# Steps, order and places of the weight conversions in a kernel of sliding-window attention and two MLPs

## The chip, the cores and the metric

The kernel runs on one core of a Trainium2 chip. Its engines work side by side, each through its own list of instructions in order: TensorE (PE) multiplies matrices, VectorE (DVE) and ScalarE (ACT) do elementwise work, SyncE (SP) issues the transfers (DMA). An instruction starts when the one before it on its engine has started its way through and the semaphores that it waits for are set. The metric is the time of one execution in device microseconds (us).

## The reference

```python
def _attn_ref(q, k, v):                     # 4 batches, 8 heads, 576 positions, 64 a head
    scores = scale * np.matmul(q, k.transpose(0, 1, 3, 2))
    mask_plain = (rel >= 0) & (rel < 32)                              # heads 0 to 3
    mask_dil = (rel >= 0) & (rel < 128) & (rel % 4 == 0)              # heads 4 to 7
    ...
    attn = np.exp(scores - max); attn = attn / (sum + 1e-09)
    return np.matmul(attn, v)

def _moe_ref(x, w_in, w_out, s, b):         # 2304 tokens, 512 -> 2048 -> 512
    r = np.maximum(x @ w_in, 0.0)
    return (s * (r * r) + b) @ w_out

def _moe2_ref(x, w_in, w_out):
    h = x @ w_in
    return (h * np.cos(h)) @ w_out
```

The attention's output, as rows of 512 numbers for each of the 2304 tokens, goes through the first MLP (`_moe_ref`) and its result through the second (`_moe2_ref`). The weights are float64 as drawn.

## The kernel before

**Tiles and steps.** The tokens lie in five tiles of 384, 384, 512, 512 and 512. The hidden 2048 numbers are 16 chunks of 128; each chunk has an in-half (128x512 of the first matrix: half 2f) and an out-half (half 2f + 1). One step p takes one chunk of one tile: p = 0 to 79 the first MLP, tile by tile, p = 80 to 159 the second. In a step TensorE makes h of the chunk (`mm_in`), then y of the chunk of two steps ago (`mm_out`); between them lie relu2 (ScalarE twice, then VectorE twice, for an exact split of its result into a high and a low part) or the cosine of the second MLP. Every product of the later tiles is three matmuls (high with high, high with low, low with high); the first tile of the first MLP is done with plain float32 matmuls on the converted weights.

**Attention.** There are 48 units (192 tokens by a pair of heads). The first eight are done in a prelude; the rest in pairs, woven into the steps of the first MLP. A pair begun at step p has its scores at the start of p, its softmax behind y at p (VectorE L238, L247, then ScalarE's exponentials L250), its normalisation at p + 1 (VectorE L261 to L263), its transposes on TensorE at the end of p + 1 (L271), and its product with v (L283) at the end of p + 2. Pairs are begun at 3, 6, 9, 12; 16, 18, 21, 23, 26, 28; 32, 34, 37, 39, 42, 44; 49, 52, 56, 59 (`DUO`).

**Weights.** A half arrives as float64 words (512 KB) in a raw place. `w_float` makes float32 of it with two ScalarE passes (L117, L118), `w_join` with four operations of VectorE (L124, L127, L130, L133). I call the two together a conversion. For the first MLP, `w_whole` does conversions in the order 0, 1, 2, ... of the halves, two a step, in the first tile (`w_point`: up to 2p + 4 at the first point of step p, behind `mm_in`, and 2p + 5 at the second, behind `mm_out`); five raw places (`stage`) are loaded three ahead. `w_split` then makes the high and the low part, a half at a time (ScalarE L139, VectorE L140), in-halves from step 13 on, out-halves from step 16 on. For the second MLP a half is loaded, converted one step later and cut into its high and low part one step after that (`w_cut`: ScalarE L147, VectorE L148, two transfers to HBM, L149 and L150), at steps spread evenly over the tiles 1 to 4; `w_fetch` brings the parts back in the last tile, the in-half at step 64 + f and the out-half at 66 + f (L155, L156).

**What sets the order.** Nothing is scheduled by a planner: under `manual_schedule` each engine's list is the order in which the code emits. In a step that is `mm_in`, the events of phase 0 (scores, normalisations), y of a tile's last chunk, `w_point` (0), relu2 or cosine, `mm_out`, `w_point` (1), fetches, events of phase 1 (softmax), of phase 2 (transposes, products with v). The second MLP's loads, conversions and cuts are events of phase 1 or 2, whichever their evenly spread position falls in, and come behind a pair's in the same phase.

Of the kernel before, what the change touches and what calls it, by code (L numbers as in the profile page):

```python
# [54 lines left out]
def attention_then_two_mlps(ctx, tc, qk_p, qk_d, v_p, v_d, mask_p, mask_d, w1, w2, sv, bv, out):  # L55
# [41 lines left out]
    def w_load(m, k, stage):  # L100
        raw_w[m, k] = stage
        nc.sync.dma_start(stage[:, :DM], (w1, w2)[m][k])

    def w_float(m, k):
        words = raw_w[m, k][:, :DM].bitcast(U32).rearrange("p (n two) -> p n two", two=2)
        low, high = words[:, :, 0], words[:, :, 1]
        if m == 0 and k + 2 < 2 * NFC:
            a = wpool.tile([P, DM], I32, tag=f"wl{k + 2}", name=f"wa{m}_{k}")
        elif m == 0:
            if not last_two:  # L110
                last_two.append(wpool.tile([P, 2, DM], I32, tag="raw2", name="last_two"))
            a = last_two[0][:, k % 2, :]
        else:
            a = late[0].tile([P, DM], I32, tag=f"wa{k % 2}", name=f"wa{m}_{k}")
        w32[m, k] = a
# [4 lines left out]
    def w_join(m, k):  # L120
        words = raw_w[m, k][:, :DM].bitcast(U32).rearrange("p (n two) -> p n two", two=2)
        low, high = words[:, :, 0], words[:, :, 1]
        a = w32[m, k]
# [19 lines left out]
    def w_cut(k):  # L143
        a = w32.pop((1, k))
        hi = raw_w.pop((1, k)).bitcast(F32R)[:, :DM]
        cut[k] = scratch.tile([P, 2, DM], F32, tag=f"cut{k}", name=f"cut{k}")
# [2 lines left out]
        nc.sync.dma_start(cut[k][:, 0, :], hi.bitcast(F32))  # L149
        nc.sync.dma_start(cut[k][:, 1, :], a.bitcast(F32))  # L150

    def w_fetch(k):
        wh[1, k] = wpool.tile([P, DM], F32R, tag=f"wh{k}", name=f"wh1_{k}")
        wl[1, k] = wpool.tile([P, DM], F32R, tag=f"wl{k}", name=f"wl1_{k}")
        nc.sync.dma_start(wh[1, k].bitcast(F32), cut[k][:, 0, :])  # L155
        nc.sync.dma_start(wl[1, k].bitcast(F32), cut[k][:, 1, :])  # L156
# [20 lines left out]
    def a_load_first(i, what):  # L177
# [6 lines left out]
        place = lambda n, shape: wpool.tile(  # L184
            shape, F32, tag=("wh", "wl")[(5 * i + n) % 2] + str(2 * NFC - 1 - (5 * i + n) // 2), name=f"first{n}_{i}"
        )
        d["place"] = place
# [493 lines left out]
```

## Time and profile before

| what | before |
|---|---|
| median of 3 runs | 925.08 us (923.73 to 925.69) |
| the profiled execution | 924.52 us, its span 922.7 us |
| TensorE busy | 895.6 us, 97% of the span |
| VectorE busy | 590.2 us, 64% |
| ScalarE busy | 507.5 us, 55% |
| HBM read and written | 75.71 and 23.07 MB |

The times in the rows below are microseconds from the start of the span. The prelude ends near 30 us, the first tile near 123, the first MLP near 515. In the chain of work that ended last, 88% of the span is TensorE's and 7% VectorE's. A bracket at a row's end is the idle time of its engine just before it, with what ended it; a row without one followed straight on.

### The profile page before, as it was taken

The numbers are of one execution on the slowest core, as the hardware profiler recorded it, in microseconds if no ns is written. First come the engines' busy times: TensorE is split into PE (matmuls) and PEld (weight loads), VectorE is DVE, ScalarE is ACT, GpSimd is POOL, SyncE is SP. The second block draws the span as 40 slices with busy tenths as digits, with TensorE's granted clock in tenths as the row PEclk, the third lists the DMA queues.
The fourth block names the chain that finished last, engine by engine and source line by source line (L and its number), as shares of the span: only waits on it lengthen the run. The fifth ranks groups of instructions, "written<-read, shape, count | busy, mean of one in ns | idle before, by whom it ended". The sixth has DMA issues, their size and how long they took to land.

```text
span 922.7 us, 13285 instructions
## 1 busy us (share of the span) xinstructions
PE 895.6 (97%) x4888; PEld 755.4 (82%) x4888; DVE 590.2 (64%) x1160; ACT 507.5 (55%) x1162; POOL 0.7 (0%) x6
## 2 busy tenths in 40 slices
PE   6899999989999989999999999999999999999998
PEld 5566679889888877778888899999988888888886
DVE  6888868666565665557464766665755665566554
ACT  5767757666564654546353654645544554454443
POOL 0000000000000000000000000000000000000000
PEclk9799999999999999999999999999999999999999
DMA  9767424332534433436799700000000010001001
GB/s 261 245 224 241 138 72 156 105 119 88 173 129 138 143 122 125 156 101 215 251 319 309 256 16 1 20 16 1 20 15 1 1 45 1 1 1 47 0 1 46
DMA packets 45536, 99.64 MB, mean 108 GB/s; under 512 B 5440, under 2 KB 12064, under 8 KB 45472
## 3 DMA queue, kind: packets, MB, share of 16 engines
q1 hardware_dynamic: 45472, 98.80, 32.1%
q8 instruction: 39, 0.64, 0.3%
q14 instruction: 25, 0.20, 0.1%
HBM read 75.71 MB, written 23.07 MB: 107 GB/s over the span
## 4 chain that ended last, share of the span: by engine, by line
PE 88%; DVE 7%; ACT 3%; issue 1%; DMA 0%; SPq 0%; DVEq 0%
PE h L332 13%; PE h L333 13%; PE h L334 13%; PE y L349 12%; PE y L350 12%; PE y L351 12%; PE y L346 4%; PE h L326 4%; PE sc L220 2%; PE pv L283 2%; ACT sm L250 2%; PE tp L271 1%; DVE wa L133 1%; DVE wa L130 1%; DVE nmax L247 1%
## 5 line engine op out<-in xcount | busy, mean ns | idle before, releaser
L332 PE MATMUL h<-xs,wh 128*128 128x512 f32 (+1 forms) x576 | 218.6, 379 | 0.0
L349 PE MATMUL y<-g,wh 128*128 128x512 f32 (+1 forms) x576 | 214.9, 373 | 0.0
L333 PE MATMUL h<-xs,wh 128*128 128x512 f32 (+1 forms) x576 | 214.9, 373 | 0.0
L334 PE MATMUL h<-xs,wl 128*128 128x512 f32 (+1 forms) x576 | 214.8, 373 | 0.0
L351 PE MATMUL y<-g,wl 128*128 128x512 f32 (+1 forms) x576 | 213.7, 371 | 0.0
L350 PE MATMUL y<-g,wh 128*128 128x512 f32 (+1 forms) x576 | 213.6, 371 | 0.0
L332 PEld LDWEIGHTS h<-xs,wh 128*128 128x128 f32 x576 | 109.0, 189 | 15.7
L334 PEld LDWEIGHTS h<-xs,wl 128*128 128x128 f32 x576 | 108.8, 189 | 15.3
L333 PEld LDWEIGHTS h<-xs,wh 128*128 128x128 f32 x576 | 109.0, 189 | 14.8
L351 PEld LDWEIGHTS y<-g,wl 128*128 128x128 f32 x576 | 108.1, 188 | 15.1
L349 PEld LDWEIGHTS y<-g,wh 128*128 128x128 f32 x576 | 108.2, 188 | 14.8
L350 PEld LDWEIGHTS y<-g,wh 128*128 128x128 f32 x576 | 108.1, 188 | 14.7
L416 ACT ACTIVATE n<-n 128x512 f32<-128x512 f32 (+1 forms) x80 | 47.2, 590 | 102.5 <-DVE n L410 102.3
L406 ACT ACTIVATE n<-h,pmagic 128x512 f32<-128x512 f32 (+1 forms) x80 | 51.6, 646 | 87.0 <-PE h L334 86.9
L407 DVE TENSOR_SCALAR n<-n 128x512 f32<-128x512 f32 (+1 forms) x80 | 32.0, 400 | 86.6 <-ACT n L406 86.5
L422 DVE SCALAR_TENSOR_TENSOR n<-n,h 128x512 f32<-128x512 f32 (+1 forms) x80 | 50.7, 633 | 55.2 <-ACT n L417 55.2
L390 ACT ACTIVATE r<-h 128x512 f32<-128x512 f32 (+1 forms) x80 | 44.1, 551 | 67.3 <-PE h L334 58.8
L250 ACT ACTIVATE sm<-sm,nmax 96x80 f32<-96x80 f32 (+1 forms) x140 | 49.5, 355 | 46.1 <-DVE nmax L247 46.1
L400 DVE CAST g<-r 128x512 fp32r<-128x512 f32 (+1 forms) x64 | 26.1, 408 | 69.0 <-ACT r L398 59.5
L124 DVE TENSOR_SCALAR wa<-wa 128x512 f32<-128x512 f32 x62 | 26.2, 423 | 42.4 <-ACT wa L117 39.7
L410 DVE SCALAR_TENSOR_TENSOR n<-n,r 128x512 f32<-128x512 f32 (+1 forms) x80 | 51.1, 638 | 2.8
L409 DVE SCALAR_TENSOR_TENSOR r<-n,h 128x512 f32<-128x512 f32 (+1 forms) x80 | 50.7, 634 | 2.8
(81 smaller groups left out, 1060.6 us busy)
## 6 DMA issues: line engine op xcount, KB each, us to landing
stage<-w SPq DMA_DIRECT2D x32, 512.0 KB, 4.7
raw<-w SPq DMA_DIRECT2D x32, 512.0 KB, 4.6
cut<-raw SPq DMA_DIRECT2D x32, 256.0 KB, 2.1
cut<-wa SPq DMA_DIRECT2D x32, 256.0 KB, 2.5
wh<-cut SPq DMA_DIRECT2D x32, 256.0 KB, 3.9
wl<-cut SPq DMA_DIRECT2D x32, 256.0 KB, 4.4
qk<-qk_d SPq DMA_DIRECT2D x20, 352.0 KB, 3.4
qk<-qk_p SPq DMA_DIRECT2D x20, 304.0 KB, 2.9
```

Of the source, the lines that this page charges most:

```text
L250: nc.scalar.activation(out=sm[:, j, :], in_=sm[:, j, :], func=AF.Exp, bias=nmax[:, j : j + 1], scale=1.0, accum_out=ssum[:, j : j + 1],)
L332: nc.tensor.matmul(h[:, : SIZES[t]], hi, x[:, 0, :], start=cc == 0, stop=False)
L333: nc.tensor.matmul(h[:, : SIZES[t]], hi, x[:, 1, :], start=False, stop=False)
L334: nc.tensor.matmul(h[:, : SIZES[t]], lo, x[:, 0, :], start=False, stop=cc == NCC - 1)
L349: nc.tensor.matmul(y[:, : SIZES[t]], hi, g[:, 0, :], start=fc == 0, stop=False)
L350: nc.tensor.matmul(y[:, : SIZES[t]], hi, g[:, 1, :], start=False, stop=False)
L351: nc.tensor.matmul(y[:, : SIZES[t]], lo, g[:, 0, :], start=False, stop=fc == NFC - 1)
L406: nc.scalar.activation(out=n, in_=h[:, : SIZES[t]], func=AF.Identity, scale=1.0 / TWO_PI, bias=pmagic)
L409: nc.vector.scalar_tensor_tensor(out=r, in0=n, scalar=-C1, in1=h[:, : SIZES[t]], op0=ALU.mult, op1=ALU.add)
L410: nc.vector.scalar_tensor_tensor(out=n, in0=n, scalar=-C2, in1=r, op0=ALU.mult, op1=ALU.add)
L416: nc.scalar.activation(out=r, in_=r, func=AF.Sin, scale=0.5)
L422: nc.vector.scalar_tensor_tensor(out=r, in0=r, scalar=-1.0, in1=h[:, : SIZES[t]], op0=ALU.add, op1=ALU.mult)
```

## The change

1. Order of the first MLP's conversions: the in-halves of the first three chunks, then out-half f together with in-half f + 3 (`W_ORDER`), still two a step and to the same counts at each point. An in-half is so converted earlier in the list, an out-half later.
2. Nine raw places (five of `stage` and the four tiles that later hold a split x) instead of five, loaded five ahead.
3. Prelude: a unit's transposes and product with v come one iteration earlier, and the loop is one shorter; the first conversion stands behind the last transposes. The three memsets of g go to the kernel's start.
4. Weight tiles hold a whole chunk. `w1_split` splits it in one ScalarE and one VectorE operation of 128x1024, at step 14 + f, ahead of relu2; 16 such splits instead of 32 of half the width. The attention's first tiles lie in the high parts' tiles.
5. The second MLP's conversions are begun in written-out steps (`BG_STEPS`), none of which begins a pair: 19, 22, 25, 30; 33, 35, 36, 38, 40, 41, 45, 47; 48, 50, 51, 53, 54, 55, 57, 58, 61, 63; 64 to 70, 72, 73, 74. Before they were 19, 23, 26, 30; 33, 35, 37, 39, 41, 43, 45, 47; 48, 50, 52, 53, 55, 56, 58, 60, 61, 63; 64, 66, 68, 69, 71, 72, 74, 76, 77, 79, of which 23, 26, 37, 39, 52 and 56 begin a pair. The load is at phase 0 of the step before, the conversion at phase 1, the cut at phase 0 of the next step, ahead of relu2.
6. A chunk's fetch is two transfers of 512 KB at step 66 + f.

```diff
-W_FIRST, W_STEPS = (7, 8, 9, 10), {8: 1, 9: 2, 11: 3}
+W_FIRST, W_STEPS = (7, 8, 9, 10), {9: 1, 10: 3}
-AHEAD = 3
+AHEAD = 5
-IN_CUT = 13
+W_ORDER = [0, 2, 4] + [k for f in range(NFC) for k in (2 * f + 1, 2 * f + 6) if k < 2 * NFC]
+CUT = 14
...
+BG_STEPS = ((), (3, 6, 9, 14), (1, 3, 4, 6, 8, 9, 13, 15), (0, 2, 3, 5, 6, 7, 9, 10, 13, 15), (0, 1, 2, 3, 4, 5, 6, 8, 9, 10))
...
-    def w_split(k):
-        a = w32.pop((0, k)).bitcast(F32)
-        wh[0, k] = wpool.tile([P, DM], F32R, tag=f"wh{k}", name=f"wh0_{k}")
-        wl[0, k] = wpool.tile([P, DM], F32R, tag=f"wl{k}", name=f"wl0_{k}")
-        nc.scalar.copy(wh[0, k], a)
-        nc.vector.tensor_tensor(out=wl[0, k], in0=a, in1=wh[0, k].bitcast(F32), op=ALU.subtract)
+    def w1_load(n, k):
+        place, tag = (stage, f"s{n % 9}") if n % 9 < 5 else (xspool, f"xs{n % 9 - 5}")
+        raw_w[k] = place.tile([P, DM], I64, tag=tag, name=f"stage{k}")
+        nc.sync.dma_start(raw_w[k], w1[k])
...
+    def w1_split(fc):
+        a = flat(w32.pop(fc)).bitcast(F32)
+        wh[0, fc] = wpool.tile([P, 2, DM], F32R, tag=f"wh{fc}", name=f"wh0_{fc}")
+        wl[0, fc] = wpool.tile([P, 2, DM], F32R, tag=f"wl{fc}", name=f"wl0_{fc}")
+        nc.scalar.copy(flat(wh[0, fc]), a)
+        nc.vector.tensor_tensor(
+            out=flat(wl[0, fc]), in0=a, in1=flat(wh[0, fc]).bitcast(F32), op=ALU.subtract
+        )
...
+    def w2_fetch(fc):
+        for w, n, l in ((wh, 0, "wh"), (wl, 1, "wl")):
+            w[1, fc] = wpool.tile([P, 2, DM], F32R, tag=f"{l}{fc}", name=f"{l}1_{fc}")
+            nc.sync.dma_start(w[1, fc].bitcast(F32), cut[fc][:, n])
...
-        def w_whole(n):
+        def w_whole(n, more=1):
...
-            while q[2] < n:
-                while q[1] < min(q[2] + 2, 2 * NFC):
+            while q[2] < n or q[1] < min(n + more, 2 * NFC):
+                while q[1] < min(q[2] + 1 + more, n + more, 2 * NFC):
                     w_load_to(q[1] + 1)
-                    w_float(0, q[1])
+                    w1_float(W_ORDER[q[1]])
                     q[1] += 1
-                w_join(0, q[2])
-                q[2] += 1
+                if q[2] < n:
+                    w1_join(W_ORDER[q[2]])
+                    q[2] += 1
...
-        for k in range(n0 + 4):
+        for k in range(n0 + 3):
             if k < n0:
                 a_scores(k, ps_a)
                 a_softmax(k)
             if 0 <= k - 1 < n0:
                 a_norm(k - 1)
+            if 0 <= k - 2 < n0:
+                a_transpose(k - 2, ps_a)
             if 0 <= k - 3 < n0:
-                a_transpose(k - 3, ps_a)
-            if 0 <= k - 4 < n0:
-                a_pv(k - 4, ps_y, f"y{k % NCC}")
+                a_pv(k - 3, ps_y, f"y{k % NCC}")
...
-                w_whole(int(W_PACE * (p + half / 2)) + WPRE)
-            if half == 0 and 0 <= p - IN_CUT < NFC:
-                w_split(2 * (p - IN_CUT))
-            if half == 1 and 0 <= p - NFC < NFC:
-                w_split(2 * (p - NFC) + 1)
+                w_whole(2 * p + half + WPRE)
+            if half == 0 and 0 <= p - CUT < NFC:
+                w1_split(p - CUT)
...
-                at((p - 1, ph), load)
-                at((p, ph), lambda k=k: w_float(1, k))
-                at((p, ph), lambda k=k: w_join(1, k))
-                at((p + 1, ph), lambda k=k: w_cut(k))
+            at((p - 1, 0), lambda k=k: w2_load(k))
+            at((p, 1), lambda k=k: w2_float(k))
+            at((p, 1), lambda k=k: w2_join(k))
+            at((p + 1, 0), lambda k=k: w2_cut(k))
...
-            f = p - NFC * (NTILE - 1)
+            f = p - NFC * (NTILE - 1) - LAG[0]
             if 0 <= f < NFC:
-                w_fetch(2 * f)
-            if 0 <= f - LAG[0] < NFC:
-                w_fetch(2 * (f - LAG[0]) + 1)
+                w2_fetch(f)
```

VectorE at the end of the prelude, before: the last row of a unit's normalisation, copies of transposes (L273) and the first two conversions (L124 to L133, on the tiles wa_0 and wa_1).

```order
L263 TENSOR_TENSOR first_7_346<-first_7_346,rec_374 96x320
L273 COPY first_5_383<-tp_378 80x384
L124 TENSOR_SCALAR wa_0_395<-wa_0_395 128x512
L127 TENSOR_SCALAR wa_0_395<-wa_0_395 128x512
L130 SCALAR_TENSOR_TENSOR wa_0_395<-stage_154,wa_0_395 128x512
L133 ISA wa_0_395<-stage_154,wa_0_395 128x1024
L273 COPY first_6_412<-tp_407 80x384
L124 TENSOR_SCALAR wa_1_398<-wa_1_398 128x512
L127 TENSOR_SCALAR wa_1_398<-wa_1_398 128x512
L130 SCALAR_TENSOR_TENSOR wa_1_398<-stage_158,wa_1_398 128x512
L133 ISA wa_1_398<-stage_158,wa_1_398 128x1024
L273 COPY first_7_438<-tp_433 80x384
```

VectorE at the same place after: normalisation (L287), copies (L297), first conversion (L112 to L121, on wa_395, which is the in-half of chunk 0).

```order
L285 TENSOR_SCALAR ssum_350<-ssum_350 96x4
L286 RECIPROCAL rec_375<-ssum_350 96x4
L287 TENSOR_TENSOR first_qk_147<-first_qk_147,rec_375 96x320
L297 COPY first_v_158<-tp_379 80x384
L297 COPY first_v_162<-tp_402 80x384
L112 TENSOR_SCALAR wa_395<-wa_395 128x512
L115 TENSOR_SCALAR wa_395<-wa_395 128x512
L118 SCALAR_TENSOR_TENSOR wa_395<-stage_152,wa_395 128x512
L121 ISA wa_395<-stage_152,wa_395 128x1024
```

The copies for the last two units stood behind the first and the second conversion; now both stand ahead of the first.

VectorE in step 26, where a pair is begun, before: maxima of the softmax (L247), the conversion of a half of the second MLP, and the first unit's normalisation (L261 to L263), which belongs to step 27.

```order
L247 TENSOR_REDUCE nmax_1992<-sm_1990 96x4
L238 SCALAR_TENSOR_TENSOR sm_1999<-sc_1955,m_d 96x320
L247 TENSOR_REDUCE nmax_2001<-sm_1999 96x4
L124 TENSOR_SCALAR wa_2_2008<-wa_2_2008 128x512
L127 TENSOR_SCALAR wa_2_2008<-wa_2_2008 128x512
L130 SCALAR_TENSOR_TENSOR wa_2_2008<-raw_1935,wa_2_2008 128x512
L133 ISA wa_2_2008<-raw_1935,wa_2_2008 128x1024
L261 TENSOR_SCALAR ssum_1994<-ssum_1994 96x4
L262 RECIPROCAL rec_2028<-ssum_1994 96x4
L263 TENSOR_TENSOR sm_1990<-sm_1990,rec_2028 96x320
```

VectorE at the same pair after.

```order
L271 TENSOR_REDUCE nmax_1916<-sm_1914 96x4
L262 SCALAR_TENSOR_TENSOR sm_1923<-sc_1878,m_d 96x320
L271 TENSOR_REDUCE nmax_1925<-sm_1923 96x4
L285 TENSOR_SCALAR ssum_1918<-ssum_1918 96x4
L286 RECIPROCAL rec_1945<-ssum_1918 96x4
L287 TENSOR_TENSOR sm_1914<-sm_1914,rec_1945 96x320
```

The four operations between the second maximum and the normalisation are gone from this place; they are at step 25.

SyncE in the last tile of the first MLP, before, in some one and a half steps: cut (L149, L150), fetches by halves (L155, L156), load of a raw half (L102).

```order
L149 DMA cut_4652<-raw_4563 128x512
L150 DMA cut_4652<-wa_24_4604 128x512
L155 DMA wh_12_4695<-cut_3533 128x512
L156 DMA wl_12_4696<-cut_3533 128x512
L155 DMA wh_9_4699<-cut_3218 128x512
L156 DMA wl_9_4700<-cut_3218 128x512
L102 DMA raw_4703<-w 128x512
L149 DMA cut_4705<-raw_4611 128x512
L150 DMA cut_4705<-wa_25_4657 128x512
```

SyncE at a like place after: load (L156), fetches by chunks (L179), cuts (L173, L174).

```order
L179 DMA wh_1_4446<-cut_1887 128x1024
L179 DMA wl_1_4448<-cut_1887 128x1024
L173 DMA cut_4421<-raw_4373 128x512
L174 DMA cut_4421<-wa_25_4450 128x512
L156 DMA raw_4474<-w 128x512
L179 DMA wh_2_4494<-cut_2400 128x1024
L179 DMA wl_2_4496<-cut_2400 128x1024
L173 DMA cut_4518<-raw_4426 128x512
L174 DMA cut_4518<-wa_26_4498 128x512
L156 DMA raw_4523<-w 128x512
```

Four fetches of 256 KB a step became two of 512 KB, and in steps that follow each other there is a load and a cut in each.

## Rows read from the trace of the kernel before

**Rows 1.** The page: busy time of TensorE, share of the span.

```profile
PE 895.6 (97%) x4888; PEld 755.4 (82%) x4888; DVE 590.2 (64%) x1160; ACT 507.5 (55%) x1162; POOL 0.7 (0%) x6
```

**Rows 2.** Waits of TensorE, whole span: total us, times, longest us.

```profile
PE tp L271 <- DVE ssum L261: 8.2, 4, 2.8
...
PE tp L271 <- DVE sm L263: 2.0, 7, 0.4
```

**Rows 3.** TensorE's timeline, the four long waits: start, duration, instruction, idle before.

```profile
174.47 0.50 PE L271 MATMUL tp<-ident,sm 96*80 96x96 f32 x4 [1.77 <-DVE ssum L261]
...
193.81 0.50 PE L271 MATMUL tp<-ident,sm 96*80 96x96 f32 x4 [2.84 <-DVE ssum L261]
...
344.63 0.62 PE L271 MATMUL tp<-ident,sm 128*96 128x128 f32 x3 [2.35 <-DVE ssum L261]
...
392.97 0.50 PE L271 MATMUL tp<-ident,sm 96*80 96x96 f32 x4 [1.29 <-DVE ssum L261]
```

**Rows 4.** VectorE's timeline around the pair of step 26.

```profile
190.41 0.43 DVE L124 TENSOR_SCALAR wa<-wa 128x512 f32<-128x512 f32 x1 [2.58 <-ACT wa L117]
...
192.78 0.16 DVE L261 TENSOR_SCALAR ssum<-ssum 96x4 f32<-96x4 f32 x1
...
193.99 0.49 DVE L263 TENSOR_TENSOR sm<-sm,rec 96x320 f32<-96x320 f32 x1
```

**Rows 5.** ScalarE at step 26; VectorE and ScalarE at the cut in step 49.

```profile
189.74 0.65 ACT L117 ACTIVATE wa<-raw 128x512 f32<-128x512 f32 x1
...
343.01 0.69 DVE L148 TENSOR_TENSOR wa<-wa,raw 128x512 fp32r<-128x512 f32 x1 [1.98 <-ACT raw L147]
...
342.38 0.60 ACT L147 CAST raw<-wa 128x512 fp32r<-128x512 f32 x1
```

**Rows 6.** Windows: stretch, PE, PEld, DVE, ACT, POOL busy, clock, DMA share, GB/s.

```profile
190.00:195.00 5.00, 1.85 (x13) 1.38 (x12) 4.24 (x12) 3.33 (x7) 0.00 (x0) 0.97 0.00 0
195.00:200.00 5.00, 5.00 (x32) 4.99 (x30) 2.78 (x7) 2.62 (x6) 0.00 (x0) 0.69 0.28 105
...
345.00:350.00 5.00, 4.83 (x18) 3.81 (x17) 3.45 (x7) 1.21 (x3) 0.00 (x0) 0.67 0.07 24
```

**Rows 7.** VectorE's timeline, from the end of the prelude to the first pair.

```profile
22.92 0.55 DVE L273 COPY first<-tp 80x384 f32<-80x384 f32 x1
23.51 0.43 DVE L124 TENSOR_SCALAR wa<-wa 128x512 f32<-128x512 f32 x1
...
29.57 0.41 DVE L124 TENSOR_SCALAR wa<-wa 128x512 f32<-128x512 f32 x1
...
51.18 0.45 DVE L238 SCALAR_TENSOR_TENSOR sm<-sc,m_p 128x288 f32<-128x288 f32 x1
...
54.86 0.46 DVE L263 TENSOR_TENSOR sm<-sm,rec 128x288 f32<-128x288 f32 x1
```

**Rows 8.** TensorE's timeline, the first h and the first pair's transposes.

```profile
30.78 9.72 PE L326 MATMUL h<-xy,wa 128*128 128x384 f32 x24
...
54.60 0.49 PE L271 MATMUL tp<-ident,sm 128*96 128x128 f32 x3
55.46 0.51 PE L271 MATMUL tp<-ident,sm 128*96 128x128 f32 x3 [0.37 <-DVE sm L263]
```

**Rows 9.** The last tile: a window, and ScalarE's timeline (a load's wait, relu2 of two steps).

```profile
500.00:510.00 10.00, 10.00 (x46) 8.28 (x45) 5.72 (x11) 5.20 (x9) 0.00 (x0) 1.00 0.97 334
...
460.91 0.66 ACT L117 ACTIVATE wa<-raw 128x512 f32<-128x512 f32 x1 [3.43 <-DMA raw<-w]
...
472.55 0.60 ACT L390 ACTIVATE r<-h 128x512 f32<-128x512 f32 x1 [2.56 <-PE h L334]
...
477.99 0.60 ACT L390 ACTIVATE r<-h 128x512 f32<-128x512 f32 x1
```

**Rows 10.** A split's two operations: count, shortest/median/longest ns, first and last start, forms.

```profile
L139 ACT CAST wh<-wa x30: 598/605/642, 111.0 to 211.5; 128x512 fp32r<-128x512 f32 x30
...
L140 DVE TENSOR_TENSOR wl<-wa,wh x30: 681/685/694, 113.1 to 212.5; 128x512 fp32r<-128x512 f32 x30
```

More of the change, by code (lines that the diff above doesn't have):

```diff
@@ L93, in attention_then_two_mlps, with words, w_float, w_join @@
     raw_w, w32 = {}, {}
-    last_two = []
     after_att = []
[L100 to L115, printed above, removed]
+    def words(raw):
+        w = raw.bitcast(U32).rearrange("p (n two) -> p n two", two=2)
+        return w[:, :, 0], w[:, :, 1]
+    def w_float(raw, a):
+        low, high = words(raw)
         nc.scalar.activation(out=a.bitcast(F32), in_=high.bitcast(F32), func=AF.Abs)
         nc.scalar.activation(out=low.bitcast(I32), in_=low, func=AF.Copy, scale=2.0**-29)
[L120 to L123, printed above, removed]
+    def w_join(raw, a):
+        low, high = words(raw)
         nc.vector.tensor_scalar(
@@ new lines, in w1_load, with w1_float, w1_join @@
+    def w1_load(n, k):
+        place, tag = (stage, f"s{n % 9}") if n % 9 < 5 else (xspool, f"xs{n % 9 - 5}")
+        raw_w[k] = place.tile([P, DM], I64, tag=tag, name=f"stage{k}")
+        nc.sync.dma_start(raw_w[k], w1[k])
+    def w1_float(k):
+        fc = k // 2
+        if fc not in w32:
+            w32[fc] = wpool.tile([P, 2, DM], I32, tag=f"wl{fc + 1}" if fc + 1 < NFC else "raw2", name=f"wa{fc}")
+        w_float(raw_w[k], w32[fc][:, k % 2, :])
+    def w1_join(k):
+        w_join(raw_w[k], w32[k // 2][:, k % 2, :])
@@ new lines, in w1_split, with w2_load @@
+    def w1_split(fc):
[6 more added lines that the diff above has]
+        )
+    def w2_load(k):
+        n = k % 2 if k < BG[1] else (k - BG[1]) % 3
+        place, tag = (late[0], f"raw{n}") if n < 2 else (wpool, "raw2")
+        raw_w["2", k] = place.tile([P, DM], I64, tag=tag, name=f"raw{k}")
+        nc.sync.dma_start(raw_w["2", k], w2[k])
@@ L147, in w_cut, with w2_float, w2_join, w2_cut @@
+    def w2_float(k):
+        w32["2", k] = late[0].tile([P, DM], I32, tag=f"wa{k % 2}", name=f"wa2_{k}")
+        w_float(raw_w["2", k], w32["2", k])
+    def w2_join(k):
+        w_join(raw_w["2", k], w32["2", k])
+    def w2_cut(k):
+        a = w32.pop(("2", k))
+        hi = raw_w.pop(("2", k)).bitcast(F32R)[:, :DM]
+        fc = k // 2
+        if fc not in cut:
+            cut[fc] = scratch.tile([P, 2, 2, DM], F32, tag=f"cut{fc}", name=f"cut{fc}")
         nc.scalar.copy(hi, a.bitcast(F32))
@@ L148, in w_cut @@
         nc.vector.tensor_tensor(out=a.bitcast(F32R), in0=a.bitcast(F32), in1=hi.bitcast(F32), op=ALU.subtract)
[L149 to L156, printed above, removed]
+        nc.sync.dma_start(cut[fc][:, 0, k % 2, :], hi.bitcast(F32))
@@ L183, in a_load_first @@
         d = st.setdefault(i, dict(dil=dil, nb=nb, nq=nq, nk=nk, tb=tb, hp=hp, b=b, u=u))
[L184 to L187, printed above, removed]
         if what == "v":
-            d["v"] = place(2, [nk, nb, P])
+            two = wpool.tile([P, 2 * DM], F32, tag=f"wh{2 * i + 1}", name=f"first_v{i}")
+            d["v"] = two[:nk, : nb * P].rearrange("p (j n) -> p j n", j=nb)
+            d["pt"] = two[:nk, 512:896]
             nc.sync.dma_start(d["v"], (v_d if dil else v_p)[b, hp % 2, u])
@@ L383, in g_tile @@
         return g
-    whole_g = []
+    whole_g = [gpool.tile([P, 2 * T], F32, tag=f"g{i}", name=f"g{i}") for i in range(3)]
+    for g in whole_g:
+        nc.vector.memset(g[:, SIZES[0] : SIZES[0] + 1], 1.0)
     def relu2(t, fc):
```

50 lines of the change are left out of this document (20 added, 30 removed).

## Prediction

> **What bounds the kernel now.** I read the share of each engine first, then the waits of TensorE, then the timelines around the longest of these waits, and last the granted clock by stretch. TensorE is busy for 895.6 us, 97% of the span [rows 1], so the time is TensorE's work plus the 27 us in which it stands still or has not begun. A change that leaves the matmuls alone can only win in those 27 us and in stretches where TensorE works at half clock. The list of its waits says where: the largest entry is transposes of attention waiting for a softmax, 8.2 us in 4 waits, with 2.0 us in 7 short ones behind them [rows 2]. The four long waits are at 174.47, 193.81, 344.63 and 392.97: 1.77, 2.84, 2.35 and 1.29 us, together 8.25 [rows 3]. These are steps 24, 27, 50 and 57, each the step behind one where a pair of units is begun. The second layer's matmuls (from 520 us on) never wait.
>
> VectorE at step 26 shows the cause. Behind the row maxima VectorE stands idle for 2.58 us until the ScalarE pass of a weight conversion (L117) is there, does the conversion's four operations, and only at 192.78 begins the normalisation for which TensorE waits [rows 4]. ScalarE starts that pass at 189.74, directly behind the pair's eight exponentials [rows 5]. So the conversion sits between softmax and normalisation on both engines: the normalisation could have begun as soon as the first unit's exponentials were done. At 343.01 the same is done by a cut (L148), which waits 1.98 us for its ScalarE half [rows 5].
>
> Two of the waits cost twice. Around the idle 2.84 and 2.35 us the granted clock is 0.97 ahead, then 0.69 and 0.67 over five microseconds [rows 6]; of two levels, 1.2 and 2.4 GHz, that is 3.1 and 3.3 us at the lower. Behind the idle 1.77 and 1.29 us TensorE's matmuls keep their length.
>
> **The change, part by part.** The sum is made against the profiled execution, 924.52 us (span 922.7); the median of the runs, 925.08, lies 0.06% above it.
>
> (1) Second layer's conversions in other steps. They are no longer begun in a step that begins a pair, so at steps 26 and 23 VectorE goes straight from the maxima to the normalisation. At step 26: exponentials end at 189.74 [rows 5], the two normalisations take 192.78 to 194.48, 0.85 us each [rows 4], so the second would end near 190.6; TensorE is there at 193.81 - 2.84 = 190.97 [rows 3]. No wait. Step 23 has the same shape and a shorter wait, 56 too. At step 49 the cut moves ahead of the softmax, but exponentials end only at 342.38, where L147 starts now [rows 5], so the second unit's normalisation ends near 343.3, and TensorE, there at 342.28, does a first transpose of 0.62 and waits some 0.4 to 0.65. Gains: 8.25 of the long waits and 1.6 of the short ones (2.0 less 0.37 at 55.46 [rows 2, 8]), less 0.5 left: 9.3 us. What is late next there is nothing on TensorE's path: a pair with no conversion beside it, four in tile 1, shows no wait. The conversion itself goes to steps without a pair, where TensorE's own work of about 5 us hides 1.3 us of ScalarE and 2.4 us of VectorE.
>
> (2) The clock behind two waits. Lost while TensorE was working: (1 - 0.69) x 5 = 1.55 and (1 - 0.67) x 5 = 1.65 [rows 6], with 0.1 each in the last of the stretch ahead: 3.4 us. If the waits go, this goes.
>
> (3) The prelude. VectorE is the bound there. Now a transpose copy (22.92), the first conversion (23.51), another copy, the second conversion and another copy follow each other, and the matmuls of h start at 30.78, when the last copy has been used [rows 7, 8]. After the change the last two copies come ahead of the first conversion: three copies from 22.92 at 0.59 each put its start near 24.4 to 24.7 (the lower if small holes in front of it close), its end 2.4 later near 27.0, and h starts at 27.0 to 27.4: about 3.5 us earlier.
>
> (4) What becomes of that head start. Behind it VectorE still has the same list: eleven conversions before the softmax of the first pair, which begins at 51.18 (nine of them from 29.57 on, 2.4 us each [rows 7]). Copies only change places with conversions, so that softmax moves by the holes that close: 0.2 to 0.65 us, to about 50.6. TensorE has 54.60 - 30.78 = 23.82 us of work before the pair's transposes [rows 8], and so is there at 51.0, while the first normalisation ends at 53.7 and the second (now 54.86 + 0.46 = 55.3 [rows 7]) at 54.7. The transposes wait 2.7 us, then 0.65. So TensorE goes on at about 55.2 instead of 55.8: 0.6 gained, not 3.5. From there to the end of the tile TensorE is the later of the two by 0.1 to 0.3 us at each pair. And 2.7 us of idleness lies with the waits that were followed by the lower clock (2.35, 2.84), not with those that were not (1.77, 1.29). I take a third fall, bounded by 0.9 and 1.7, at 1.4. Net: -0.6 + 1.4 = +0.8; without the fall -0.6.
>
> (5) Order and places of the first layer's weights. Two conversions a step before and after; an in-half is converted earlier, an out-half one step later and still two steps ahead of its use. Nine raw places only let loads lead further. Cost nothing: hidden behind TensorE's steps; if the cover went, it would be a wait for one conversion, 2.4 us.
>
> (6) Splits by chunk: 16 of 128x1024 instead of 32 of 128x512. No row shows that width. One split of 512 takes 605 ns on ScalarE and 685 on VectorE [rows 10]; the wide one lies between once and twice that. I take near twice, 1.1 and 1.2, since it has twice the elements. It stands ahead of relu2 now, for 1.1 us in a path with some 8 us to spare (below). Zero on TensorE, bounded by 0 and 1 us over the tile.
>
> (7) Last tile of the first layer: fetches come as whole chunks two steps later than the first halves did, and ten conversions lie in steps 64 to 74 instead of 64 to 79. In steps 66 to 74 the queue is given 9 fetches of 1.05 MB, 7 loads and 8 cuts of 0.52 MB: 17.3 MB. A step is 477.99 - 472.55 = 5.44 us [rows 9], nine are 49 us: 353 GB/s are asked for. The row shows 334 at a busy share of 0.97 [rows 9], which gives 51.8 us, 2.8 us behind at the end. A load has 1.5 steps (8.2 us) before ScalarE wants it, and behind ScalarE's wait relu2 has two steps less its own 2.5, 8 us, before TensorE wants its result; already ScalarE waits 3.43 us for such a load at 460.91 [rows 9] and TensorE does not feel it. So nothing.
> The Trainium skill, DMA: Bandwidth & Descriptors, Specifications, gives about 358 GB/s as a core's limit at HBM; the row's 334 agrees with it from below. By the page the backlog would be none, by the row 2.8 us, and either way the sum is the same; the rival of a starved last tile would lose a part of its chance by the page.
>
> Sum: 924.5 - 9.3 - 3.4 + 0.8 = 912.6; I say **912.5 us**.
>
> **The rivals.** A: the head start is kept. If the first pair's softmax on VectorE came about 3 us earlier than I have it, part (4) gives -3.5 instead of +0.8: 908.3. For it: h really starts earlier. Against it: the conversions queue ahead of the softmax in VectorE's order, in the same number. A milder form, no fall of the clock, gives 911.2.
>
> B: waits stay in pair steps. A cut now stands ahead of relu2 and of a pair's softmax in its step, and a wide split can lie ahead of a normalisation; if half of the 9.3 us came back that way, and one fall of the clock with it, the time is 912.6 + 4.65 + 1.7 = 919. Against it: worked through, steps 23, 26 and 56 have their normalisation in time by 0.3 us or more. For it: at step 26 that is all the room there is.
>
> C, slower: the last tile starves. One mechanism: 17.3 MB asked for in 49 us, ScalarE waits for loads, relu2 queues behind it, TensorE stops. It starts when the backlog passes the load's room (8.2 less its usual 4.6 to land) plus 8, that is 11.6 us, at a rate under 17.3 / 60.6 = 286 GB/s; it eats the whole gain of 12 us at about 17.3 / 73 = 237, and at 230 the time is 927. Against it: 334 is shown with the same kinds of transfer in the same tile.
>
> **How the numbers follow.** Forecast 0.63 (its own range 910.5 to 914.5, from the clock falling or not, and the bounds of 4 and 6), A 0.12, B 0.20, C 0.05. The range, 908.0 to 919.5, takes in A and most of B. A measurement of this kernel tells about 0.2% (1.9 us) from no change. A, the forecast and B are faster by more than that, but for an end of B at full return of the waits: faster 0.90, same 0.05, slower 0.05.
>
> **What would show it.** In the trace after: no wait of a transpose over 0.7 us between 120 and 420; no fall of the clock near 195 and 345; h starting near 27; a wait of about 2.7 us of the first pair's transposes near 53.5 with a lower clock behind it; ScalarE waiting for loads near 470 to 490 with TensorE busy. Wrong if the pair near 53.5 does not wait (A), if transposes wait elsewhere (B), or if TensorE waits for relu2 in the last tile (C).

## The result, and the profile after

The changed kernel takes 913.43 us, median of 5 runs (911.95 to 915.29), against 925.08 (923.73 to 925.69): a ratio of 0.9877, 95% interval 0.9859 to 0.9894. The profiled execution has a span of 910.6 us instead of 922.7. The forecast was 912.5 with a range of 908.0 to 919.5.

The page after, the line of busy times (share of the span, instructions) and TensorE's granted clock in 40 slices, in tenths, answering [rows 1]:

```profile
PE 894.2 (98%) x4888; PEld 755.1 (83%) x4888; DVE 593.2 (65%) x1144; ACT 507.9 (56%) x1146; POOL 0.7 (0%) x6
...
PEclk9899999999999999999999999999999999999999
```

TensorE's instructions are the same 4888. Its busy time is 1.4 us shorter, and the time in which it stands still or has not begun 10.7 us. Its waits after, whole span, answering [rows 2]:

```profile
PE sc L244 <- DMA first_qk<-qk_p: 4.3, 2, 3.5
PE tp L295 <- DVE sm L287: 3.7, 4, 2.4
PE tp L295 <- ACT first_qk L274: 2.4, 4, 1.1
PE h L350 <- DVE wa L121: 1.3, 1, 1.3
PE tp L295 <- ACT xy L325: 0.6, 1, 0.6
```

The entry of 8.2 us in [rows 2], transposes waiting for a softmax's sum, is gone. What stands in its place are 3.7 us in four waits, of which 2.37 and 0.57 are at the first pair of the first tile, the head start turned into a wait that the prediction spoke of, and 0.16 and 0.57 at the pair of step 49.

Where the time went is read from the starts of h in each step on TensorE's two timelines. This table has every step at which the difference changes by more than 0.4 us (the first row is the start of steps 0 to 2, which follow in one piece):

| step | h begins, before | after | difference | change there |
|---|---|---|---|---|
| 0 | 30.78 | 28.27 | -2.51 | -2.51 |
| 5 | 55.80 | 56.37 | +0.57 | +2.93 (+0.15 at step 3) |
| 6 | 61.91 | 63.99 | +2.07 | +1.51 |
| 25 | 175.57 | 175.44 | -0.14 | -2.43 (+0.22 at step 24) |
| 28 | 195.10 | 191.36 | -3.74 | -3.60 |
| 29 | 203.30 | 198.19 | -5.11 | -1.37 |
| 39 | 263.69 | 257.88 | -5.81 | -0.70 |
| 51 | 345.92 | 337.58 | -8.34 | -2.13 |
| 52 | 353.53 | 344.06 | -9.46 | -1.12 |
| 54 | 367.19 | 357.01 | -10.18 | -0.71 |
| 58 | 394.07 | 381.97 | -12.10 | -1.94 |

From step 58 to the end nothing changes any more. So tile 0 lost 2.1 us, and tiles 1 to 3 won 14.2.

### The profile page after: what moved, and what is told of

It reads as the page before. It is cut to its first block, busy times and chain, and to the rows that moved or that the text cites. A ratio compares the mean times of both kernels' runs of the same rounds, so it can differ in the third digit from the quotient of the medians.

```text
span 910.6 us, 13169 instructions
## 1 busy us (share of the span) xinstructions
PE 894.2 (98%) x4888; PEld 755.1 (83%) x4888; DVE 593.2 (65%) x1144; ACT 507.9 (56%) x1146; POOL 0.7 (0%) x6
## 4 chain that ended last, share of the span: by engine, by line
PE 94%; DVE 3%; ACT 2%; DMA 1%; issue 1%; SPq 0%; DVEq 0%
PE h L356 13%; PE h L357 13%; PE h L358 13%; PE y L373 13%; PE y L375 13%; PE y L374 13%; PE h L350 5%; PE y L370 4%; PE sc L244 3%; PE pv L307 2%; PE tp L295 2%; ACT sm L274 1%; DMA stage<-w 1%; DVE nmax L271 0%; DMA first_qk<-qk_p 0%
## 5 line engine op out<-in xcount | busy, mean ns | idle before, releaser
L375 PE MATMUL y<-g,wl 128*128 128x512 f32 (+1 forms) x576 | 213.7, 371 | 0.0
L374 PE MATMUL y<-g,wh 128*128 128x512 f32 (+1 forms) x576 | 213.6, 371 | 0.0
L374 PEld LDWEIGHTS y<-g,wh 128*128 128x128 f32 x576 | 108.2, 188 | 14.9
L375 PEld LDWEIGHTS y<-g,wl 128*128 128x128 f32 x576 | 108.1, 188 | 15.0
L453 DVE TENSOR_TENSOR g<-n,g 128x512 fp32r<-128x512 f32 (+1 forms) x80 | 50.4, 630 | 0.7 <-ACT g L452 0.7
```

The source lines that it names most:

```text
L374: nc.tensor.matmul(y[:, : SIZES[t]], hi, g[:, 1, :], start=False, stop=False)
L375: nc.tensor.matmul(y[:, : SIZES[t]], lo, g[:, 0, :], start=False, stop=fc == NFC - 1)
L453: nc.vector.tensor_tensor(out=g[:, 1, :], in0=r, in1=g[:, 0, :].bitcast(F32), op=ALU.subtract)
```

## The experiments

Theory: the twelve microseconds are the second layer's conversions leaving the pair's steps, waits and falls of the clock together; the first layer's rearrangement brings nothing, since its head start runs into VectorE's list. Rivals: the splits by chunk or the new order of the first layer carry a part; the clock has no price of its own. The kernels were run four at a time beside the kernel before on one chip; its medians were 924.85 (undo_steps, steps_only, prelude_back, two_fewer), 926.6 (filled_wait, conv_in_26, conv_in_23, best) and 924.9 (the other four), so ratios stand beside the times. The runs of one kernel spread over 1.4 to 5.4 us. Differences of medians below some 3 us are therefore not settled by the medians; for these I read the starts of steps, in one trace of each kernel.

### The steps of the second layer, taken back and taken alone

undo_steps, the changed kernel with the old steps and phases:

```diff
-        for k, p in enumerate(t * NFC + step for t, steps in enumerate(BG_STEPS) for step in steps):
-            at((p - 1, 0), lambda k=k: w2_load(k))
...
+                b = t * NFC + (2 if t == 1 else 0) + (i + 0.5) * (NFC - (2 if t == 1 else 0)) / n
+                p, ph = int(b), 1 + int(b % 1 >= 0.5)
+                at((p - 1, ph), lambda k=k: w2_load(k))
...
```

> The changed kernel with the second layer's conversions back in their evenly spread steps and phases; all of the first layer's changes stay. By the times at which steps begin, the change gained 14.2 us between steps 24 and 58 and lost 2.1 us between steps 3 and 6. If the gain is the steps' alone (theory): 913.4 + 14.2 = 927.6 us, with the four long waits of transposes back (8 to 9 us) and two falls of the clock near 195 and 345. If a part of the gain comes from the splits by chunk or the raw places (rival): 920 or less, with waits that are shorter.

Measured: 925.84 us, ratio 1.0009 (0.9993 to 1.0025): the whole gain is gone. By the interval the first layer's changes together are worth something between 0.6 us won and 2.3 us lost; in the traces they lose 1.8 us in tile 0 and win 1.5 back in tiles 1 to 3. Its trace, waits of TensorE, then the transpose of step 27, then the window behind it (columns as in [rows 6]):

```profile
PE tp L295 <- DVE ssum L285: 5.9, 3, 2.3
...
PE tp L295 <- ACT raw L171: 1.2, 1, 1.2
```

```profile
194.42 0.50 PE L295 MATMUL tp<-ident,sm 96*80 96x96 f32 x4 [2.23 <-DVE ssum L285]
```

```profile
195.00:200.00 5.00, 4.77 (x26) 4.79 (x27) 3.97 (x6) 2.96 (x6) 0.00 (x0) 0.66 0.28 105
```

The four long waits are back, 7.1 us in all, and the clock falls again behind this one. They are 1.2 us shorter than in [rows 2]: 2.23 instead of 2.84 here and 1.18 instead of 1.77 at step 24 [rows 3], 0.6 each, about the length of a half's split (0.685 us [rows 10]); with splits by chunk one that stood ahead of the pair's softmax in VectorE's list is no longer there.

steps_only, the kernel before with nothing but the new steps:

```diff
+BG_STEPS = ((), (3, 6, 9, 14), (1, 3, 4, 6, 8, 9, 13, 15), (0, 2, 3, 5, 6, 7, 9, 10, 13, 15), (0, 1, 2, 3, 4, 5, 6, 8, 9, 10))
...
-                at((p - 1, ph), load)
-                at((p, ph), lambda k=k: w_float(1, k))
-                at((p, ph), lambda k=k: w_join(1, k))
-                at((p + 1, ph), lambda k=k: w_cut(k))
...
+        for k, p in enumerate(t * NFC + step for t, steps in enumerate(BG_STEPS) for step in steps):
...
+            at((p - 1, 0), load)
+            at((p, 1), lambda k=k: w_float(1, k))
+            at((p, 1), lambda k=k: w_join(1, k))
+            at((p + 1, 0), lambda k=k: w_cut(k))
```

> The kernel before with nothing but the new steps and phases of the second layer's conversions. Theory: 925.1 - 14.2 = 910.9 us, 2 us under the changed kernel, no wait of a transpose over 0.7 us from 120 us on, first h at 30.8. Rival (the splits by chunk or the order of the first layer are needed for it): 914 or more, with waits left at steps 24, 27, where splits of halves stand between.

Measured: 912.41 us, ratio 0.9864 (0.9846 to 0.9882). That is 12.4 us gained by the steps alone, 1.5 less than expected, and no wait of a transpose over 0.6 us is left. The 12.4 us agree with the loss of undo_steps (925.84 - 913.43 = 12.4). Its waits of TensorE, the entries of tiles 0 to 3:

```profile
PE tp L272 <- DVE sm L264: 1.3, 4, 0.6
PE h L333 <- DVE sm L239: 0.7, 1, 0.7
```

The second is h at step 24, behind a half's split in VectorE's list; the kernels with splits by chunk wait 0.15 us there. The expectation had put all of the 14.2 us of tiles 1 to 3 down to the steps. In the traces they win 13.3 there alone (steps_only beside before) and 12.7 beside undo_steps; the rest is the splits' share. Nor did h begin at 30.8: it begins at 33.30, though this prelude is the one of before. That comes back below.

### The first tile: head start, wait, clock

prelude_back, the changed kernel with the old prelude:

```diff
-W_FIRST, W_STEPS = (7, 8, 9, 10), {9: 1, 10: 3}
+W_FIRST, W_STEPS = (7, 8, 9, 10), {8: 1, 9: 2, 11: 3}
...
-        for k in range(n0 + 3):
+        for k in range(n0 + 4):
...
-            if 0 <= k - 2 < n0:
-                a_transpose(k - 2, ps_a)
             if 0 <= k - 3 < n0:
-                a_pv(k - 3, ps_y, f"y{k % NCC}")
-            if k == n0:
-                w_whole(0)
+                a_transpose(k - 3, ps_a)
+            if 0 <= k - 4 < n0:
+                a_pv(k - 4, ps_y, f"y{k % NCC}")
```

> The changed kernel with the prelude of before (transposes and products with v one iteration later, first conversion ahead of the last two copies). Theory: the loss of 2.1 us near step 4 is the earlier start of h turned into a wait of 2.4 us and a fall of the clock; with the start back at 30.8 the wait is under 0.5, the clock stays, 911.3 us. Rival (the new order of conversions or the nine places slow the first tile): the loss stays, 913.4.

Measured: 910.57 us, ratio 0.9843 (0.9826 to 0.9859). In its trace h begins at 31.82, 3.6 us later than in the changed kernel, and by step 6 it is 0.6 ahead: the wait is 0.36 us and the clock from 55 to 60 is 1.00, as expected. By the medians alone it is not clear of the changed kernel, whose repeat below has the ratio 0.9857.

two_fewer:

```diff
-WPRE = 4
+WPRE = 2
```

> The changed kernel with two conversions fewer ahead of each point of the first tile (2p + 2 and 2p + 3 instead of 2p + 4 and 2p + 5), which the new order allows. Theory: the first pair's softmax begins 4.7 us earlier, at 46.9, so its transposes do not wait, no fall of the clock near 55: the wait (2.37 + 0.57 us) and the 1.5 us behind it go, 913.4 - 4.4 = 909.0. Rival (VectorE bounds the whole tile, so the wait only moves to the next pair or to y): 912 to 914, with waits at 70 to 115 us.

Measured: 909.4 us, ratio 0.9833 (0.9809 to 0.9857). TensorE's timeline at the first pair, and the window behind it, of two_fewer:

```profile
52.39 0.82 PE L295 MATMUL tp<-ident,sm 128*96 128x128 f32 x6
```

```profile
55.00:60.00 5.00, 5.00 (x38) 3.06 (x37) 4.45 (x10) 3.71 (x8) 0.00 (x0) 1.00 0.29 111
```

Six transposes in one piece, no bracket, clock 1.00. Step 5 begins 3.3 us earlier than in the changed kernel, step 6 4.8, and nothing is given back later: the conversions that are put off fit in behind the last pair. It was the number of conversions ahead of the softmax that ate the head start, not VectorE's total.

filled_wait, 13 more transposes of the identity in the idle time:

```diff
+FILL = 13
...
+        if i == 8:
+            for _ in range(FILL):
+                nc.tensor.transpose(acc[:, :P], ident, ident)
         for j in range(nb):
```

> The changed kernel with 13 more transposes of the identity on TensorE, ahead of the first pair's transposes and into the same PSUM place, which these overwrite: some 2.1 us of work in its idle 2.4 us, nothing else moved. Theory (the idle time makes the clock fall, and the fall costs by itself): clock 1.00 from 55 to 60 where the changed kernel has 0.66, the transposes end as before, step 6 begins 1.5 us earlier, 911.9 us. Rival (the loss at step 6 has another cause, as VectorE's or the loads' lateness): the same 913.4.

Measured: 911.96 us, ratio 0.9841 (0.9821 to 0.9861). The same place in the changed kernel and in filled_wait, each with TensorE's timeline and the window:

```profile
54.77 0.50 PE L295 MATMUL tp<-ident,sm 128*96 128x128 f32 x3 [2.37 <-DVE sm L287]
55.85 0.73 PE L295 MATMUL tp<-ident,sm 128*96 128x128 f32 x3 [0.57 <-DVE sm L287]
...
55.00:60.00 5.00, 4.43 (x13) 2.63 (x12) 4.62 (x11) 4.80 (x10) 0.00 (x0) 0.66 0.25 75
```

```profile
52.26 1.58 PE L297 MATMUL tp<-ident 128*128 128x128 f32 x13
54.91 0.50 PE L299 MATMUL tp<-ident,sm 128*96 128x128 f32 x3 [1.06 <-DVE sm L288]
55.98 0.50 PE L299 MATMUL tp<-ident,sm 128*96 128x128 f32 x3 [0.57 <-DVE sm L288]
...
55.00:60.00 5.00, 4.43 (x18) 2.75 (x19) 4.62 (x11) 4.97 (x11) 0.00 (x0) 1.00 0.18 55
```

The pair's transposes end within 0.1 us of each other, and only the clock differs, 0.66 against 1.00. Step 6 begins 1.56 us earlier with the fill. In this pair of traces that is the price of one fall by itself; work that does nothing made the stretch shorter.

after_again, the changed kernel unchanged:

> The changed kernel once more, beside the next three on one chip. Its profile of the first time had a fall of the clock behind a wait of 2.4 us near 55; two other kernels with the same first tile waited 1.75 and 1.89 us there without one. If the fall comes and goes from run to run, its times spread over some 1.5 us more than those of a kernel without the wait: 911.5 to 915, median 913.4.

Measured: 912.16 us (910.58 to 913.79), ratio 0.9857 (0.9833 to 0.9881). Here the first tile went another way. The transposes of the first pair and the window, of after_again:

```profile
57.78 0.51 PE L295 MATMUL tp<-ident,sm 128*96 128x128 f32 x3 [1.68 <-DVE sm L287]
...
55.00:60.00 5.00, 2.74 (x13) 1.54 (x12) 4.13 (x13) 4.42 (x17) 0.00 (x0) 1.00 0.65 249
```

h begins at 31.21 instead of 28.27, so the wait is 1.68 us and the clock does not fall. Three microseconds of head start less cost 1.3 at step 6, because with them went a part of the wait and the fall. The times did spread as the expectation said, but not for its reason: two runs take 910.6 us and two 913.7, and the traced one, of 913.79, has no fall at 55. What the two shorter ones did otherwise is not traced.

### One conversion put back into a pair's step

conv_in_26 and conv_in_23:

```diff
-BG_STEPS = ((), (3, 6, 9, 14), (1, 3, 4, 6, 8, 9, 13, 15), (0, 2, 3, 5, 6, 7, 9, 10, 13, 15), (0, 1, 2, 3, 4, 5, 6, 8, 9, 10))
+BG_STEPS = ((), (3, 6, 10, 14), (1, 3, 4, 6, 8, 9, 13, 15), (0, 2, 3, 5, 6, 7, 9, 10, 13, 15), (0, 1, 2, 3, 4, 5, 6, 8, 9, 10))
```

and in conv_in_23 (3, 7, 9, 14) in the same place.

> The changed kernel with one conversion of the second layer (the third) begun in step 26, which begins a pair, instead of 25. Theory: the wait of before comes back there alone, 2.8 + 0.3 us idle, 0.4 for starting again, and a fall of the clock behind it of 1.4: 913.4 + 4.9 = 918.3. Without a price for the clock (rival): 916.5.

> The changed kernel with one conversion of the second layer (the second) begun in step 23 instead of 22. Theory: an idle time of 1.8 us and 0.3 behind it, 0.3 for starting again, and no fall of the clock, since before had none here: 913.4 + 2.4 = 915.8. If any idle time of this kind makes the clock fall (rival): 917.3.

Measured: 914.12 us, ratio 0.9867 (0.9846 to 0.9888), and 914.87 us, ratio 0.9872 (0.9847 to 0.9897). The transposes, of conv_in_26 with the window behind them, then of conv_in_23:

```profile
192.69 0.50 PE L295 MATMUL tp<-ident,sm 96*80 96x96 f32 x4 [2.23 <-DVE ssum L285]
...
195.00:200.00 5.00, 5.00 (x51) 4.74 (x50) 4.79 (x10) 2.84 (x9) 0.00 (x0) 1.00 0.51 159
```

```profile
176.95 0.50 PE L295 MATMUL tp<-ident,sm 96*80 96x96 f32 x4 [1.18 <-DVE ssum L285]
```

One conversion in a pair's step is enough to bring a wait back at that place alone: step 28 begins 2.8 us later in the one, step 25 1.8 us in the other. The rest stays, but for 0.46 us more at step 28 of conv_in_23, where the second unit's transposes wait 0.37 us. So the mechanism holds. The sizes missed: the waits are 2.23 and 1.18, not 2.84 and 1.77, for the split that is gone (above), and the clock did not fall behind 2.23 us here, though it did behind the same 2.23 us in undo_steps. The medians cannot tell either kernel from the changed one, whose two ratios are 0.9877 and 0.9857.

### The last tile, loaded harder

fetch_more:

```diff
-            nc.sync.dma_start(w[1, fc].bitcast(F32), cut[fc][:, n])
+            for _ in range(2 - n):
+                nc.sync.dma_start(w[1, fc].bitcast(F32), cut[fc][:, n])
```

> The changed kernel with each high part fetched twice in the last tile: 1.57 MB of fetches a step instead of 1.05. Theory (the last tile has room for a backlog of some 11.6 us in all): in steps 66 to 74 22.0 MB are asked for in 49 us; at the 334 GB/s of the rows that takes 65.9, a backlog of 16.9, of which TensorE loses some 5: 918.7, with ScalarE's waits for loads first and TensorE waiting for relu2 behind them. Rival (loads get through beside the fetches, or there is more room): 913.4.

Measured: 936.16 us, ratio 1.0119 (1.0093 to 1.0146): slower than before. Its waits of ScalarE and of TensorE between 420 and 560 us, that of SyncE between 430 and 540, and two windows:

```profile
ACT wa L107 <- DMA raw<-w: 34.5, 6, 13.0
...
PE y L374 <- DVE g L425: 12.6, 4, 5.8
...
SPq L180 <- DMA wh<-cut: 68.4, 11, 7.6
```

```profile
480.00:490.00 10.00, 10.00 (x39) 8.09 (x38) 0.46 (x1) 0.00 (x0) 0.00 (x0) 0.83 0.83 286
490.00:500.00 10.00, 4.15 (x14) 2.77 (x13) 4.05 (x7) 2.98 (x5) 0.00 (x0) 0.86 0.71 251
```

The end of rival C's chain is there: ScalarE waits up to 13.0 us for a load, relu2 queues behind it, and TensorE waits for relu2. Its beginning is another. SyncE stands for 68.4 us in 11 waits at L180, the fetch, until a fetch of a high part has landed: the second transfer into the same place waits for the first, and the cuts and loads behind it in SyncE's list wait with it. So the loads were issued late, and the queue moved 251 to 286 GB/s at a share of 0.71 to 0.83, not 334, being given its transfers that much later. The run therefore does not test a full queue, nor the room of 11.6 us. The size was missed by a factor of four: its span is 24.0 us longer than that of after_again. TensorE's waits for relu2 are 13.1 us of that (12.6 at L374, 0.5 at L375), and some 10 are the lower clock (an estimate from the granted clock of 0.71 to 0.86 in the five windows of 10 us from 470 to 520).

### Kernels beyond the change

best, two_fewer with the pair of step 49 begun at 50:

```diff
-DUO = ((), (3, 6, 9, 12), (0, 2, 5, 7, 10, 12), (0, 2, 5, 7, 10, 12), (1, 4, 8, 11))
+DUO = ((), (3, 6, 9, 12), (0, 2, 5, 7, 10, 12), (0, 2, 5, 7, 10, 12), (2, 4, 8, 11))
...
-BG_STEPS = ((), (3, 6, 9, 14), (1, 3, 4, 6, 8, 9, 13, 15), (0, 2, 3, 5, 6, 7, 9, 10, 13, 15), (0, 1, 2, 3, 4, 5, 6, 8, 9, 10))
+BG_STEPS = ((), (3, 6, 9, 14), (1, 3, 4, 6, 8, 9, 13, 15), (0, 1, 3, 5, 6, 7, 9, 10, 13, 15), (0, 1, 2, 3, 4, 5, 6, 8, 9, 10))
```

> Two conversions fewer ahead of each point of the first tile, and the pair of step 49 begun at 50 with the conversion of step 50 at 49, so that the pair's softmax no longer stands in the step in which the tile's y is written out. Theory: the 0.17 + 0.57 us that its transposes wait near 336 go: 909.4 - 0.8 = 908.6. Rival (the pair at 52 follows too close and waits, or the conversion at 49 does): 909.4 or more.

Measured: 908.81 us, ratio 0.9803 (0.9776 to 0.983). The two waits near 336 are gone in the trace, where the steps behind gained 1.1 us over two_fewer. The medians, 0.6 apart, do not settle it.

best_prelude_back, the same with the old prelude (edit as above):

> The kernel with two conversions fewer ahead and the pair at 50, and with the prelude of before. Theory: h began 2.5 to 3 us later with that prelude in the runs so far; with the full number of conversions ahead this head start was lost at the first pair, with two fewer it is kept, so it must be missing here: 908.8 + 2.5 = 911.3. Rival (the head start is worth nothing in either): 908.8.

Measured: 909.25 us, ratio 0.9829 (0.9809 to 0.9849): not the 2.5 us more that the theory wanted. In its trace h begins at 30.43, in that of best at 31.24, and this difference stays to the end. But the two traces are not alike at the start: best's score groups take 1.57 us up to the last, at 21.94, and those of best_prelude_back 0.9 us from 11.40 on, which moves h by itself (see the prelude below). So what the prelude's order or a head start is worth with two conversions fewer is left open by this pair.

best_pool, best with a multiplication of the prelude on GpSimd:

```diff
-        nc.vector.tensor_tensor(out=d["sm"], in0=d["sm"], in1=rec.to_broadcast([nr, nb, nk]), op=ALU.mult)
+        (nc.gpsimd if i < 8 else nc.vector).tensor_tensor(out=d["sm"], in0=d["sm"], in1=rec.to_broadcast([nr, nb, nk]), op=ALU.mult)
```

> The kernel with two conversions fewer ahead and the pair at 50, and with the multiplication of the normalisation of the prelude's eight units on GpSimd, which stands idle, instead of VectorE. VectorE bounds the prelude with 2.2 us a unit, 0.41 of it this operation. Theory: eight times 0.41, less what ScalarE's exponentials and copies (1.9 us a unit) bind then: 2 us earlier, 906.8. Rival (GpSimd is slower by so much that the transposes wait for it): 909 to 914.

Measured: 907.37 us (906.43 to 910.34), ratio 0.9809 (0.9781 to 0.9838), the lowest median of all, though best has the lower ratio. The operation there, from the groups by line of best_pool (count, busy us, mean ns):

```profile
L287 POOL TENSOR_TENSOR first_qk<-first_qk,rec 128x288 f32<-128x288 f32 (+1 forms) x8 | 5.5, 691 | 18.9 <-DVE rec L286 18.9
```

GpSimd takes 691 ns for what takes VectorE 460 to 490, and TensorE's transposes wait for it three times, 2.8 us in all. h begins at 29.87, 1.4 us before that of best, but here the score groups become short between 16 and 18 us and in best none is short. Of the kernels with VectorE's normalisation in which they become short between 16 and 18 us too, undo_steps begins h at 29.65 and conv_in_23 at 29.20. So a gain by GpSimd is not shown, and the expected 2 us are not there.

## Why the prediction was right, point by point

**The mechanism and its size.** Long waits 8.25 plus short ones, less what stays at step 49, and two falls of the clock: 9.3 + 3.4 = 12.7 us were forecast for the new steps. The steps alone measure 12.4 us, both ways. Step 49 kept 0.16 + 0.57 us, 0.5 was said.

**Splits by chunk.** Put at zero with a bound of 1 us lost. Their operations last, of the changed kernel (count, shortest/median/longest ns):

```profile
L146 ACT CAST wh<-wa x16: 1028/1050/1075, 114.5 to 200.1; 128x1024 fp32r<-128x1024 f32 x16
...
L147 DVE TENSOR_TENSOR wl<-wa,wh x16: 1218/1225/1226, 118.2 to 201.2; 128x1024 fp32r<-128x1024 f32 x16
```

1.05 and 1.22 us against 1.1 and 1.2. In the sum zero was right; but where a conversion stays in a pair's step they shorten the wait by 0.6 us, which the prediction did not see.

**The prelude, the step that failed.** Terms 3 and 4 gave h at 27.0 to 27.4, the pair's first transposes at 53.7 and a net of +0.8 us. The trace has 28.27, 54.77 and +2.07. The fall was sized well (1.51 against 1.4). The failing step is that VectorE bounds the prelude by itself. TensorE's score matmuls there, of the changed kernel, of its repeat, and of steps_only, which has the old prelude, with its first h; they are the same eight instructions, one unit apart:

```profile
12.86 1.57 PE L244 MATMUL sc<-first_qk 128*96 128x80 f32 x8
...
15.50 0.91 PE L244 MATMUL sc<-first_qk 128*96 128x80 f32 x8
```

```profile
12.96 1.57 PE L244 MATMUL sc<-first_qk 128*96 128x80 f32 x8
...
15.94 1.57 PE L244 MATMUL sc<-first_qk 128*96 128x80 f32 x8
...
21.90 1.57 PE L244 MATMUL sc<-first_qk 128*96 128x80 f32 x8
```

```profile
19.99 1.57 PE L221 MATMUL sc<-first,first 128*96 128x80 f32 x8
...
33.30 10.22 PE L327 MATMUL h<-xy,wa 128*128 128x384 f32 x24
```

As long as they take 1.57 us instead of 0.91, VectorE waits for scores: 0.16 and 0.80 us in the changed kernel, and 0.73, 0.70 and 0.70 more in the repeat, where all of them are long. That is where the missing microsecond of the head start went. The old prelude waits the same way: in the trace of before the score matmuls are short from 10.47 on and h begins at 30.78, in steps_only they are long to the last and h begins at 33.30. So -2.51 in the table compares two starts that differ in more than the change. Where the score matmuls are long to the last in both, the new prelude begins h at 31.21 (after_again) against 33.30 (steps_only), a head start of 2.1 us where 3.5 was forecast. The holes in VectorE's list did close, as I had it: the eleven conversions follow each other from 25.69 to 51.57. But they began 1 us late, and with them the softmax, at 51.57 and not 50.6. VectorE around the first conversion and the first pair, of the changed kernel, answering [rows 7]:

```profile
25.69 0.41 DVE L112 TENSOR_SCALAR wa<-wa 128x512 f32<-128x512 f32 x1
...
51.57 0.45 DVE L262 SCALAR_TENSOR_TENSOR sm<-sc,m_p 128x288 f32<-128x288 f32 x1
...
55.25 0.46 DVE L287 TENSOR_TENSOR sm<-sm,rec 128x288 f32<-128x288 f32 x1
```

**Two errors that cancel.** In the traces tile 0 lost 1.3 us more than forecast, and tiles 1 to 3 gained 14.2 instead of 12.7. That the sum came out within 1 us is in part luck. Most of the 1.5 is a price that the sum did not have: a wait costs TensorE 0.3 to 0.4 us more than the idle time in its bracket. At step 25 2.43 us were won for idle times of 1.77 and 0.32, at step 58 1.94 for 1.29 and 0.32, at steps 39 and 54 0.70 and 0.71 for 0.28 each, which is 1.5 over in all. Two of the short waits, from TensorE's timeline of before:

```profile
175.29 0.50 PE L271 MATMUL tp<-ident,sm 96*80 96x96 f32 x4 [0.32 <-DVE sm L263]
...
263.43 0.51 PE L271 MATMUL tp<-ident,sm 128*96 128x128 f32 x3 [0.28 <-DVE sm L263]
```

The splits by chunk are no part of this excess, because the forecast counted the old waits whole.

**The last tile.** Windows of the changed kernel and ScalarE's wait for loads between 420 and 520:

```profile
450.00:460.00 10.00, 10.00 (x46) 8.27 (x45) 6.33 (x11) 4.72 (x8) 0.00 (x0) 1.00 1.01 389
460.00:470.00 10.00, 10.00 (x46) 8.29 (x45) 5.94 (x11) 4.23 (x7) 0.00 (x0) 1.00 0.94 321
470.00:480.00 10.00, 10.00 (x46) 8.28 (x45) 6.20 (x11) 4.63 (x8) 0.00 (x0) 1.00 0.96 360
480.00:490.00 10.00, 10.00 (x46) 8.29 (x45) 6.84 (x12) 5.36 (x10) 0.00 (x0) 1.00 0.96 320
...
ACT wa L107 <- DMA raw<-w: 6.1, 4, 3.8
```

TensorE is busy throughout, and the loads' longest wait is 3.8 us, 3.43 in [rows 9]. The backlog stayed far inside the room, as forecast; 389 and 360 GB/s were moved in two stretches, more than the 334 that I reckoned with.
The Trainium skill, DMA: Bandwidth & Descriptors, Specifications, puts a core's limit at HBM at about 358 GB/s. The 389 and 360 of these windows count reads and writes together; the windows from 27 to 35 us, in which there are only loads, show 369 and 412:

```profile
27.00:32.00 5.00, 3.73 (x6) 2.18 (x7) 4.58 (x9) 4.87 (x9) 0.00 (x0) 0.50 1.03 369
30.00:35.00 5.00, 5.00 (x13) 2.74 (x13) 4.59 (x9) 3.83 (x8) 0.00 (x0) 0.79 1.02 412
```

So in this case the page's figure is passed by 3% and by 15%, and the measurement decides.

**The rivals.** A (head start kept) did not come in the change, but it came in two_fewer, with the condition named for it: the softmax earlier in VectorE's list. B did not come: the largest wait left in tiles 1 to 3 is 0.57 us. C did not come. fetch_more does not show where it would, since its queue was held back by SyncE's list; the rate at which C begins stays an estimate.

## What to carry to other kernels

Before a background job is moved, look at which instruction stands directly behind it on each in-order engine: work spread evenly over time costs most where it lands between a producer and the consumer for which the bounding engine waits, and moving it one step away from there was the whole gain that the runs can tell from nothing. An earlier start of the bounding engine is worth only what its next rendezvous allows: count the work queued ahead of that rendezvous on the other engine, and move that too. A wait of the bounding engine is priced with what comes behind it; filling it with idle work tells the clock's share in one run.
